# Which operand stands still in the heads' product: x as weights, 64 key columns moving

## The chip, the cores and the metric

The kernel runs on one core of a Trainium2 chip. The metric is the device time of one execution in microseconds (us); three runs of the kernel before lie at 771.75, 772.20 and 772.58 us, so its time is their median, 772.2 us. A difference of 0.2% (1.5 us) is about what a measurement of this kernel can tell from no change. Durations below come from one profiled execution, which took 773.23 us, and in which the span from the first to the last instruction was 771.4 us.

## The reference

Eight batches, each of 3200 tokens and 256 columns. First a gated attention unit, then a token-mixing MLP on its output:

```python
scores = scale * np.matmul(z, z.transpose(0, 2, 1))      # z: 3200 x 64 in each batch
attn = np.maximum(scores, 0.0) ** 2
x = u * np.matmul(attn, v)                               # 3200 x 256
wq = x @ w_q ; wk = x @ w_k                              # 3200 x 64 each
W_tok = scale2 * np.einsum('bsd,btd->bst', wq, wk)
mixed = np.einsum('bst,btd->bsd', W_tok, x)              # 3200 x 256
out = np.maximum(mixed, 0.0) @ w_out
```

`W_tok` is never made. `mixed` is `wq @ (wk.T @ x)`, and the inner product `wk.T @ x`, a 64x256 matrix for each batch, summed over its 3200 tokens, is what the kernel calls the heads (tile `hs`). The change is about how this small matrix is summed.

## The kernel before

**Work of one batch.** The 3200 tokens are 25 tiles of 128 rows. They are also grouped (`widths`) into six groups of 512 columns and one of 128. `scores` (L307) multiplies z with z into a PSUM tile of two banks (`sc`). VectorE or ScalarE takes it to SBUF with the ReLU (L321, L319), GpSimd or ScalarE squares it into `at` (L332, L330). Because the attention matrix is symmetric, part of it is not computed twice but turned by DMA (`tt`, `ts`, L351). `second_product` multiplies these tiles with v into two PSUM banks `acc0`, `acc1`. `gate` (L488) multiplies by u, which gives x of the group, in fp16. Then x is turned by DMA (`xT_sb`, L518), projected to queries and keys (`projections`, PSUM tile `qk`, copied to SBUF by ScalarE, L544), and the keys are turned by DMA into `kx` (L551): 128 tokens on the partitions, the 64 key columns beside 64 columns of zeros. `heads` multiplies keys and x, tile by tile.

**Two lanes.** Nearly all products contract over 128 rows, and the kernel runs them as two halves of 64 rows (`LOW`, `HIGH`) on the two halves of the TensorE array, called lanes here. `first_pass` gives one PSUM bank to each lane, and `second_pass` swaps the banks, so that each bank gets both halves of its rows. Class `Streams` puts the items of both lanes into one order by the columns that each lane has already moved; `swap_after` makes the second pass wait for the end of the first. In the trace these matmuls have the form 64*128 (64 rows, 128 weight columns), and a helper emits them all from L369.

**Phases.** The main loop goes in phases of some 4 us. A phase computes up to three score tiles, a share of a group's second product, and at most one more job: a mix (L622), an output projection (`fo`), or `keys_and_heads`. That last one takes one `qk` tile of two banks. Bank 0 gets the projection of a new group (two items of 512 columns in each pass). Bank 1 gets the heads of an earlier group (four items of 256 columns in each pass; five when the last, small group is among them), and sometimes the mix or the output projection of the small group (`side`), or the projection of the small group. So one lane moves 1024 columns while the other moves 1024 to 1536, and the passes swap them. `uneven` compares the two banks' columns: at the beginning of a group, banks of equal width run their two passes back to back ahead of the second product; banks of unequal width have the first pass of the second product between their own two passes. Inside a group the two passes always lie apart, with second-product work between them.

**After the product.** When the passes are done, `after` lets ScalarE copy the projections (L544) and calls `heads_out`: for the first group VectorE copies the 64x256 sum to `ha` (L576), for the next it adds (L578), and for the last it adds into the fp16 tile `hs` (L591). At the end of that phase `spread_heads` has ScalarE copy `hs` from partitions 0 to 63 to partitions 64 to 127 (L586) and into `hz` (L587), since the mix reads it on both lanes. The first mix that reads a batch's `hs` comes at least two phases later: the mix just after it in the order still belongs to the batch before.

**What sets the order.** The schedule is written by hand (`manual_schedule`): the order in which the Python code emits instructions is the order on each engine. PSUM has three tiles of two banks (pool `pps`) that `sc`, `qk`, `fo` and `mx` share in turn; the buffer given back first is handed out first. A tile's first matmul waits until the last reader of that buffer's earlier tile is done.

Of the kernel before, what the change touches and what calls it, by code (L numbers as in the profile page):

```python
# [9 lines left out]
FP16 = mybir.dt.float16  # L10
FP32 = mybir.dt.float32
# [5 lines left out]
def kernel(  # L17
# [10 lines left out]
    nc = tc.nc  # L28

    B, S, D = u.shape  # L30
    dqk = z.shape[2]
    dh = moe_w_q.shape[1]
    P = 128
# [292 lines left out]
    def second_stage(p0, g, on_act):  # L326
        at = pat.tile([P, 2 * W], FP16, tag="at", name="at")
        out = at[:].rearrange("p (a w) -> p a w", a=2)
        if on_act:
            nc.scalar.square(out=out, in_=g[:])  # L330
        else:
            nc.gpsimd.tensor_mul(out=out, in0=g[:], in1=g[:])  # L332
        blocks, turns = [], []
        for h, (b, gi, tis) in enumerate(tiles[p0 : p0 + 2]):
            for i, ti in enumerate(tis):
                made[b, gi, ti] = (at, h * W + i * widths[gi])
            gj = group_of(tis[0])
            if is_turned(gi, gj) or (gj == LASTG and gi in FOR_SMALL):
                blocks.append((b, gi, gj, tis[0] - starts[gj] // P, 1, h * W, (h + 1) * W))
        if len(blocks) == 2 and blocks[0][:3] == blocks[1][:3] and blocks[1][3] == blocks[0][3] + 1:  # L340
            blocks = [blocks[0][:4] + (2, blocks[0][5], blocks[1][6])]
        for b, gi, gj, n0, nn, c0, c1 in blocks:
            if gj == LASTG:
                turned[b, gi, gj] = ptt.tile([P, 1, 4, P], FP16, tag=f"ts{gi}", name=f"ts{gi}")
            elif (b, gi, gj) not in turned:
                home = tt_of[b, gi, gj]
                turned[b, gi, gj] = ptt.tile([P, 4, 4, P], FP16, tag=f"tt{home}", name=f"tt{home}")
            out = turned[b, gi, gj][:].rearrange("p n j t -> p (n j) t")
            turns.append(
                lambda out=out[:, 4 * n0 : 4 * (n0 + nn), :], c0=c0, c1=c1:  # L350
                nc.sync.dma_start_transpose(out=out, in_=at[:, c0:c1])  # L351
            )
        return turns
# [75 lines left out]
    def run(streams, asides_):  # L429


        todo = streams.ordered()
        total, done = sum(x[0] for x in todo), [0, 0]
        asides_ = sorted(asides_, key=lambda x: x[0])
        for n, lane, fn in todo:
            while asides_ and asides_[0][0] * total <= sum(done):
                asides_.pop(0)[1](int(done[1] < done[0]))
            fn()
            done[lane] += n
        for _, fn in asides_:  # L440
            fn(0)
# [114 lines left out]
    def swapped(gi):  # L556
        return gi % 2 == 1 or gi == LASTG

    def heads(b, gis, ps, stop=True):

        parts = [(gi, n) for gi in gis for n in range(widths[gi] // P)]
        return [
            Item(
                out=ps[:, 1, 0:D],
                lhsT=lambda r, gi=gi, n=n: ks[b, gi][r, n, :, :].rearrange("p a h -> p (a h)"),
                rhs=lambda r, gi=gi, n=n: xs[b, gi][r, n, :],
                start=((gi, n) == parts[0]),
                stop=(stop and (gi, n) == parts[-1]),
            )
            for gi, n in parts  # L570
        ]

    def heads_out(b, gis, ps):
        if gis[0] == 0:
            hacc[b] = psml.tile([P, D], FP32, tag="ha", name="ha", bufs=1)
            nc.vector.tensor_copy(out=hacc[b][0:dh, :], in_=ps[0:dh, 1, 0:D])  # L576
        elif gis[-1] < LASTG:
            nc.vector.tensor_add(  # L578
                out=hacc[b][0:dh, :], in0=hacc[b][0:dh, :], in1=ps[0:dh, 1, 0:D]
            )  # L580
        else:
            heads_done(b, ps[:, 1, 0:D], spread=False)
            to_spread.append(b)

    def spread_heads(b):
        nc.scalar.copy(out=hss[b][dh:P, :], in_=hss[b][0:dh, :])  # L586
        nc.scalar.copy(out=hz[b % 2][dh:P, :], in_=hss[b][0:dh, :])  # L587

    def heads_done(b, part, spread=True):
        hss[b] = psml.tile([P, D], FP16, tag="hs", name="hs")  # L590
        nc.vector.tensor_add(out=hss[b][0:dh, :], in0=hacc.pop(b)[0:dh, :], in1=part[0:dh, :])  # L591
        if spread:
            nc.vector.tensor_copy(out=hss[b][dh:P, :], in_=hss[b][0:dh, :])
# [158 lines left out]
    to_load = []  # L752
    todo_mix, todo_proj, todo_between, at_phase, side = [], [], [], {}, []
    keyed, keyed_at, to_turn, to_spread, asides = [], [-9], [], [], []

    def due(k, fn):
        at_phase.setdefault(k, []).append(fn)
# [19 lines left out]
    def keys_and_heads(b, gis):  # L777

        ps = ps_tile("qk")
        outs = [ps[:, 0, 0:W], ps[:, 1, D : D + P]]  # L780
        w = wkq if swapped(gis[0]) else wqk
        banks = [projections(b, gis[0], w, outs[0]), []]
        aside = None
        late = len(groups) <= NG
        heads_of = keyed[: late or len(keyed) == 2]
        if late and len(keyed) == 2 and keyed[0][0] == keyed[1][0]:
            heads_of = [(keyed[0][0], keyed[0][1] + keyed[1][1])]
            keyed[:2] = heads_of
        full = len(heads_of) == 1
        if full:  # L790
            banks[1] += heads(*heads_of[0], ps, stop=(len(gis) == 1 and not side))
            if len(gis) > 1:
                banks[1] += projections(b, gis[1], w, outs[1], start=False)
            elif side:
                aside = side.pop(0)
                banks[1] += aside[0](aside[2], ps)
        assert full or len(gis) == 1

        def after():
            for gi, o in zip(gis, outs):  # L800
                projections_out(b, gi, o)
                turn_keys(b, gi)
            if full:
                hb, hgis = keyed.pop(0)
                heads_out(hb, hgis, ps)
                if hgis[-1] == LASTG:
                    mixed_at[0] = max(mixed_at[0], now[0] - 1)
                    todo_mix.extend((hb, i, db) for i in range(LASTG // 2) for db in range(ND))
                    side.append((side_mix, side_mix_out, hb))
            if aside:  # L810
                aside[1](aside[2], ps)
            keyed.append((b, gis))
            keyed_at[0] = now[0]

        return banks, after
# [120 lines left out]
    def each(fns):  # L936
        for fn in fns:
            fn()
# [40 lines left out]
    while groups:  # L979
# [108 lines left out]
        if on_lanes:  # L1088
# [50 lines left out]
            todo = [(x, lambda lead, p0=p0: stage(p0, scores(p0, lead))) for x, p0 in zip(at_, between_)]  # L1139
            for x in acts[1:]:  # L1140
                todo.append((0.5 - 1e-6, lambda lead, x=x: each(second_stage(*x))))
            run(streams, todo)
        else:
            assert not is_split(b, gi)
# [14 lines left out]
                each(second_stage(*x))  # L1159
            for fn in matmuls[cut:]:  # L1160
                fn()
        each(late)
        ahead = []
        if closes:
# [136 lines left out]
```

## Time and profile before

| | |
|---|---|
| median of three runs | 772.2 us (771.75 to 772.58) |
| the profiled execution | 773.23 us, span 771.4 us, granted TensorE clock 0.998 |
| TensorE matmul (PE) | 760.0 us busy, 99% of the span, 12440 matmuls |
| weight loads (PEld) | 621.0 us, 81%, 12440 |
| VectorE, ScalarE, GpSimd | 466.2 (60%), 549.8 (71%), 540.2 us (70%) |
| heads' product, four-tile groups (`qk<-x_sb,kx`) | 364 matmuls, 269 ns each as recorded |
| heads' copy and adds on VectorE (L576, L578, L591) | 8 at 412 ns, 30 at 411 ns, 7 at 409 ns (and one more in the last batch) |
| spread of `hs` on ScalarE (L586, L587) | 7 at 402 ns and 7 at 398 ns |

How to read it: PE matmuls are pipelined, and the recorded 269 ns of a 256-column matmul are mostly latency; what a matmul costs is the step from its start to the start of the next one on the same lane. So PE's 99% says that it hardly waits, and not that nothing in it can be made shorter. A timeline row merges instructions of one kind; its first number is the start in us from the beginning of the span, the second the time from the first start to the last end, and x gives their number.

### The profile page before, as it was taken

The numbers are of one execution on the slowest core, as the hardware profiler recorded it, in microseconds if no ns is written. First come the engines' busy times: TensorE is split into PE (matmuls) and PEld (weight loads), VectorE is DVE, ScalarE is ACT, GpSimd is POOL, SyncE is SP. The second block draws the span as 40 slices with busy tenths as digits, with TensorE's granted clock in tenths as the row PEclk, the third lists the DMA queues.
The fourth block names the chain that finished last, engine by engine and source line by source line (L and its number), as shares of the span: only waits on it lengthen the run. The fifth ranks groups of instructions, "written<-read, shape, count | busy, mean of one in ns | idle before, by whom it ended". The sixth has DMA issues, their size and how long they took to land.

```text
span 771.4 us, 28170 instructions
## 1 busy us (share of the span) xinstructions
PE 760.0 (99%) x12440; PEld 621.0 (81%) x12440; DVE 466.2 (60%) x450; ACT 549.8 (71%) x649; POOL 540.2 (70%) x354
## 2 busy tenths in 40 slices
PE   8999999999999999999999999999999999999996
PEld 6777878788788888888888887888878888888884
DVE  6655675646765667555675557655566565765534
ACT  7566776677767867687776777768677686776555
POOL 7888797768767678666787668866688666764540
PEclk9999999999999999999999999999999999999999
DMA  8899889887999979998799997999499995889637
GB/s 169 172 197 218 198 193 179 185 172 151 201 186 216 245 140 212 204 245 189 204 189 216 227 210 156 172 235 271 118 232 203 259 225 121 176 201 191 175 74 260
DMA packets 289612, 150.19 MB, mean 195 GB/s; under 512 B 265168, under 2 KB 268752, under 8 KB 289488
## 3 DMA queue, kind: packets, MB, share of 16 engines
q1 hardware_dynamic: 288768, 146.48, 91.4%
q0 software_dynamic: 576, 1.64, 1.2%
q8 instruction: 97, 1.59, 0.9%
q14 instruction: 27, 0.22, 0.1%
q10 hardware_dynamic: 144, 0.26, 0.1%
HBM read 59.38 MB, written 26.21 MB: 111 GB/s over the span
## 4 chain that ended last, share of the span: by engine, by line
PE 97%; DVE 1%; issue 0%; DMA 0%; ACT 0%; POOL 0%; SPq 0%; ACTq 0%; DVEq 0%
PE acc L369 71%; PE sc L307 12%; PE qk L369 6%; PE fo L369 5%; PE mx L622 1%; DVE x_sb L507 1%; DMA z<-in_z_dram 0%; DVE g L321 0%; PE ztp L130 0%; PE xtx L599 0%; PE hd L609 0%; ACT g L319 0%; ACT fo L1263 0%; DVE fo L1259 0%; PE qq L369 0%
## 5 line engine op out<-in xcount | busy, mean ns | idle before, releaser
L321 DVE TENSOR_SCALAR g<-sc 128x1024 f32<-128x1024 f32 x330 | 401.7, 1223 | 243.2 <-PE sc L307 223.1
L332 POOL TENSOR_TENSOR at<-g 128x1024 f16<-128x1024 f32 x230 | 433.6, 1895 | 136.0 <-DVE g L321 113.5
L369 PE MATMUL acc<-v_sb,at 64*128 64x256 f16 (+1 forms) x7187 | 462.9, 269 | 1.5 <-DVE x_sb L507 0.5
L369 PEld LDWEIGHTS <-at 64*128 64x128 f16 (+1 forms) x7187 | 355.8, 94 | 86.8 <-PE acc L369 24.6
L330 ACT ACTIVATE at<-g 128x1024 f16<-128x1024 f32 x226 | 234.9, 1055 | 15.8 <-DMA tt<-at 8.7
L369 PE MATMUL acc<-v_sb,tt 64*128 64x256 f16 x2552 | 180.7, 269 | 0.0
L307 PE MATMUL sc<-zT 64*128 64x512 f16 (+1 forms) x1008 | 165.9, 357 | 1.4 <-ACT g L319 1.3
L319 ACT ACTIVATE g<-sc 128x1024 f32<-128x1024 f32 x126 | 129.0, 1024 | 46.5 <-PE sc L307 41.4
L369 PEld LDWEIGHTS <-tt 64*128 64x128 f16 x2552 | 130.6, 94 | 15.2
L509 POOL TENSOR_TENSOR x_sb<-gt,u_sb 128x512 f16<-128x512 f32 x48 | 61.2, 1275 | 66.2 <-ACT gt L506 58.9
L643 ACT ACTIVATE rt<-mx 128x1024 f16<-128x1024 f32 x47 | 47.9, 1024 | 34.2 <-PE mx L622 34.0
L506 ACT COPY gt<-acc 128x512 f32<-128x512 f32 x48 | 28.1, 586 | 48.6 <-PE acc L369 46.8
L307 PEld LDWEIGHTS <-zT 64*128 64x128 f16 x1008 | 52.4, 94 | 10.8 <-issue 4.2
L369 PE MATMUL fo<-wo,rt 64*128 64x256 f16 (+1 forms) x696 | 58.6, 270 | 0.0
L544 ACT CAST qk<-qk 128x512 f16<-128x512 f32 x47 | 27.5, 586 | 42.2 <-PE qk L369 39.2
L369 PE MATMUL qk<-x_sb,kx 64*128 64x256 f16 (+1 forms) x364 | 54.7, 269 | 0.0
L369 PEld LDWEIGHTS <-rt 64*128 64x128 f16 (+1 forms) x696 | 36.4, 94 | 15.0 <-PE fo L369 6.3
L507 DVE TENSOR_TENSOR x_sb<-acc,u_sb 128x512 f16<-128x512 f32 x48 | 33.2, 691 | 19.9 <-PE acc L369 19.0
L704 ACT ACTIVATE fo<-fo 128x1024 f32<-128x1024 f32 x39 | 40.0, 1026 | 2.3 <-PE fo L369 2.2
L369 PEld LDWEIGHTS <-kx 64*128 64x128 f16 (+1 forms) x382 | 35.4, 94 | 6.3 <-PE qk L369 1.2
L369 PE MATMUL qk<-xT_sb,wqk 64*128 64x512 f16 (+1 forms) x92 | 27.3, 377 | 0.0
L369 PE MATMUL qk<-xT_sb,wkq 64*128 64x512 f16 (+1 forms) x90 | 26.7, 376 | 0.0
(81 smaller groups left out, 265.6 us busy)
## 6 DMA issues: line engine op xcount, KB each, us to landing
u_sb<-in_u_dram SPq DMA_DIRECT2D x48, 512.0 KB, 5.1
out_dram<-fo SPq DMA_DIRECT2D x43, 512.0 KB, 3.6
piece<-in_v_dram SPq DMA_DIRECT2D x42, 512.0 KB, 5.2
piece<-in_z_dram SPq DMA_DIRECT2D x7, 512.0 KB, 5.6
tt<-at SPq DMA_TRANSPOSE x162, 5.0
out_dram<-fo SPq DMA_DIRECT2D x9, 256.0 KB, 3.4
piece<-in_z_dram SPq DMA_DIRECT2D x7, 288.0 KB, 4.5
u_sb<-in_u_dram SPq DMA_DIRECT2D x8, 128.0 KB, 3.8
```

The source lines that it names most:

```text
L307: nc.tensor.matmul(out=sc[:, h, at : at + w], lhsT=zT[b][half : half + dqk, ds(z_at(b, h) + ti * P, P)], rhs=zT[b][half : half + dqk, ds(z ...
L319: nc.scalar.activation(out=g[:], in_=sc[:], func=RELU, scale=GSCALE)
L321: nc.vector.tensor_scalar(out=g[:], in0=sc[:], scalar1=0.0, scalar2=GSCALE, op0=AOP.max, op1=AOP.mult)
L330: nc.scalar.square(out=out, in_=g[:])
L332: nc.gpsimd.tensor_mul(out=out, in0=g[:], in1=g[:])
L369: return nc.tensor.matmul(out=self.out, lhsT=self.lhsT(rows), rhs=self.rhs(rows), start=start, stop=stop)
L506: nc.scalar.copy(out=upper[:], in_=accs[1][:])
L507: nc.vector.tensor_mul(out=x[:, 0:n], in0=accs[0][:, 0:n], in1=ug[:, 0:n])
L509: nc.gpsimd.tensor_mul(out=x[:, n : 2 * n], in0=upper[:], in1=ug[:, n : 2 * n])
L544: nc.scalar.copy(out=qks[b, gi][:, 0:gw], in_=out)
L643: nc.scalar.activation(out=out, in_=ps[:], func=RELU)
L704: nc.scalar.mul(out=flat_out[:, sl], in_=part, mul=FINAL_SCALE)
```

## The change

In all batches but the last (`b < last`) the operands of the heads' product change places. For each token tile x is the weights, in two blocks of 128 columns (`cc`), and the 64 key columns move. The output is then x's columns on the partitions and the heads on the free axis: 128 partitions, two blocks of 64 columns. `ha` becomes 128x128. For the last groups of a batch VectorE adds the sum twice into an fp16 tile `hT`, once for each of two copies of the 64 columns (`t`). A new function `turn_heads` multiplies `hT` by the identity, two products of 128 rows, 128 weight columns and 128 moving columns, which puts the heads on partitions 0 to 63 and again on 64 to 127. They go into columns 256 to 511 of the same `qk` tile's second bank, and ScalarE copies the 128x256 result to `hs`. `turn_heads` is put at the end of the phase's stream of second-product items. `spread_heads` keeps only the copy to `hz`. The last batch is computed as before.

```diff
     def heads(b, gis, ps, stop=True):
         parts = [(gi, n) for gi in gis for n in range(widths[gi] // P)]
+        if b < last:
+            return [
+                Item(
+                    out=ps[:, 1, ds(cc * dh, dh)],
+                    lhsT=lambda r, gi=gi, n=n, cc=cc: xs[b, gi][r, n, ds(cc * P, P)],
+                    rhs=lambda r, gi=gi, n=n: ks[b, gi][r, n, 0, :],
+                    start=((gi, n, cc) == parts[0] + (0,)),
+                    stop=(stop and (gi, n, cc) == parts[-1] + (ND - 1,)),
+                )
+                for gi, n in parts
+                for cc in range(ND)
+            ]
         return [
...
     def heads_out(b, gis, ps):
+        cols, n = (P, ND * dh) if b < last else (dh, D)
+        part = ps[0:cols, 1, 0:n]
         if gis[0] == 0:
-            hacc[b] = psml.tile([P, D], FP32, tag="ha", name="ha", bufs=1)
-            nc.vector.tensor_copy(out=hacc[b][0:dh, :], in_=ps[0:dh, 1, 0:D])
+            hacc[b] = psml.tile([P, n], FP32, tag="hT" if b < last else "ha", name="ha", bufs=1)
+            nc.vector.tensor_copy(out=hacc[b][0:cols, :], in_=part)
         elif gis[-1] < LASTG:
-            nc.vector.tensor_add(
-                out=hacc[b][0:dh, :], in0=hacc[b][0:dh, :], in1=ps[0:dh, 1, 0:D]
-            )
-        else:
-            heads_done(b, ps[:, 1, 0:D], spread=False)
-            to_spread.append(b)
+            nc.vector.tensor_add(out=hacc[b][0:cols, :], in0=hacc[b][0:cols, :], in1=part)
+        else:
+            hT = psml.tile([P, ND, 2, dh], FP16, tag="h16", name="hT")
+            for t in range(2):
+                nc.vector.tensor_add(
+                    out=hT[:, :, t, :],
+                    in0=hacc[b][:].rearrange("p (a h) -> p a h", a=ND),
+                    in1=part.rearrange("p (a h) -> p a h", a=ND),
+                )
+            hacc.pop(b)
+            hTs[b] = hT
+
+    def turn_heads(b, hT, ps):
+        for cc in range(ND):
+            nc.tensor.matmul(
+                out=ps[:, 1, ds(D + cc * P, P)],
+                lhsT=hT[:, cc, :, :].rearrange("p t h -> p (t h)"),
+                rhs=ident[:],
+                start=(cc == 0),
+                stop=(cc == ND - 1),
+            )
+        hss[b] = psml.tile([P, D], FP16, tag="hs", name="hs")
+        nc.scalar.copy(out=hss[b][:], in_=ps[:, 1, D : 2 * D])
+        to_spread.append(b)
 
     def spread_heads(b):
-        nc.scalar.copy(out=hss[b][dh:P, :], in_=hss[b][0:dh, :])
-        nc.scalar.copy(out=hz[b % 2][dh:P, :], in_=hss[b][0:dh, :])
+        nc.scalar.copy(out=hz[b % 2][dh:P, :], in_=hss[b][dh:P, :])
...
     def keys_and_heads(b, gis):
         assert full or len(gis) == 1
+        if full and heads_of[0][0] < last and heads_of[0][1][-1] == LASTG:
+            assert not aside and len(gis) == 1
+            hb_ = heads_of[0][0]
+            to_turn_heads.append(lambda: turn_heads(hb_, hTs.pop(hb_), ps))
...
             for x in acts[1:]:
                 todo.append((0.5 - 1e-6, lambda lead, x=x: each(second_stage(*x))))
+            if to_turn_heads:
+                streams.aside(max(streams.at), to_turn_heads.pop(0))
             run(streams, todo)
...
             for fn in matmuls[cut:]:
                 fn()
+        while to_turn_heads:
+            to_turn_heads.pop(0)()
         each(late)
```

More of the change, by code (lines that the diff above doesn't have):

```diff
@@ L754 @@
     keyed, keyed_at, to_turn, to_spread, asides = [], [-9], [], [], []
+    hTs, to_turn_heads = {}, []
     def due(k, fn):
```

## The prediction

> **What bounds the kernel now.** I read the page first, then who waits on PE, then the timeline of PE in narrow windows, since the change is about matmuls of a shape that the kernel does not have yet.
>
> ```profile
> PE 760.0 (99%) x12440; PEld 621.0 (81%) x12440; DVE 466.2 (60%) x450; ACT 549.8 (71%) x649; POOL 540.2 (70%) x354
> ...
> PE 97%; DVE 1%; issue 0%; DMA 0%; ACT 0%; POOL 0%; SPq 0%; ACTq 0%; DVEq 0%
> ...
> L369 PE MATMUL qk<-x_sb,kx 64*128 64x256 f16 (+1 forms) x364 | 54.7, 269 | 0.0
> ```
>
> The chain that ends last is PE for 97%. The longest entry of PE in the view of waits is 1.3 us in all. So whatever the two lanes save or lose is the kernel's time, nearly one to one. What a matmul costs is the step to the next one on its lane:
>
> ```profile
> 84.13 0.60 PE L307 MATMUL sc<-zT 64*128 64x128 f16 x10
> 84.57 0.60 PE L369 MATMUL acc<-v_sb,at 64*128 64x256 f16 x8
> ...
> 86.31 0.38 PE L307 MATMUL sc<-zT 64*128 64x512 f16 x2
> 86.54 1.48 PE L369 MATMUL acc<-v_sb,at 64*128 64x256 f16 x24
> 87.86 0.60 PE L369 MATMUL acc<-v_sb,tt 64*128 64x256 f16 x8
> 88.30 0.38 PE L307 MATMUL sc<-zT 64*128 64x512 f16 x2
> ```
>
> From 86.54 to 87.86, 12 pairs (one matmul on each lane): 110 ns a step; the single start times of the trace give 109. In the row at 84.13 the ten are four pairs of 128 columns and one of 512: 0.44 us less 0.216 for the 512 leaves 56 ns a step, and each of these steps also loads new weights on both lanes. The line through 109 at 256 and 56 at 128 columns gives 29.5 ns at 64. At 86.31 the step after 512 columns is 0.23 instead of 0.216: by the start times 228 against 216 where the next weights were not loaded ahead, and the recorded time of the matmul after it is 280 instead of 269. So a weight load that nothing hides costs 12 to 23 ns.
>
> ```profile
> 676.99 0.38 PE L369 MATMUL qk<-xT_sb,wqk 64*128 64x512 f16 x1
> 677.12 0.28 PE L369 MATMUL qk<-x_sb,kx 64*128 64x256 f16 x1
> 677.21 0.38 PE L369 MATMUL qk<-xT_sb,wqk 64*128 64x512 f16 x1
> 677.24 0.38 PE L369 MATMUL qk<-x_sb,kx 64*128 64x256 f16 x2
> 677.42 0.27 PE L369 MATMUL acc<-v_sb,at 64*128 64x256 f16 x1
> ```
>
> The lanes are independent: the second projection starts 215 ns after the first though heads emitted ahead of it are not started, and the lane that is through with its share goes on with the second product (677.42). So a shorter heads' share is not lost to the longer projection beside it, as long as there is second-product work behind it, and over the two passes each lane gets the short share once.
>
> **What the change removes.** 25 tiles in 7 batches, 175 tiles, each once on each lane. A tile's share of a lane is 109 ns now, and two matmuls of step t after: 109 - 2t saved, 175 times. Bounds for t: from below 29.5, the line above, weights loaded in the shadow of 64 columns. From above 29.5 + 23 = 52.5, no load hidden, or 56, the narrowest step that the trace shows. Saved: 8.75 us at 29.5; 0.7 us at 52.5; -0.5 us at 56. I take 32: the load of 12 to 23 ns fits into the 27 ns that 64 columns take at the line's slope, the other lane then needs a load only every 109 or 215 ns, and a few first loads of a run will be late. 109 - 64 = 45 ns, 175 times: **7.9 us saved**.
>
> The Trainium skill speaks against that: its page "TensorE: Matmul & The Clock Gate", section LDWEIGHTS, gives a load 1/1.2 ns for each weight column, 107 ns for 128 whatever the rows, and its section on weight-path modes reports about half of that as measured with fast weight load. By 53 ns a load the step would be bound at some 53 to 56 ns and the sum would come out near +2.6 us, the loss priced below as a rival. The trace excludes 107 (a step with a load on each lane in 56 ns), and cannot exclude 53.
>
> **What it adds on PE.** `turn_heads`, seven times: two 128-row matmuls of 128 columns, 56 ns each. They stand among 64-row matmuls, and that switch has a price:
>
> ```profile
> 52.16 0.38 PE L307 MATMUL sc<-zT 64*128 64x512 f16 x2
> 52.47 0.60 PE L369 MATMUL qk<-xT_sb,wqk 128*128 128x512 f16 x2
> 53.01 0.39 PE L307 MATMUL sc<-zT 64*128 64x512 f16 x2
> ```
>
> 0.31 us from a 512-column pair to the 128-row matmul, against 0.216: 97 ns by the start times, and the same back (0.54 less 0.43). 2 x 0.056 + 2 x 0.097 = 0.31 us, seven times 2.1 us. Does PE also wait for `hT`? Two ends of the tail after the heads:
>
> ```profile
> 331.66 0.59 ACT L544 CAST qk<-qk 128x512 f16<-128x512 f32 x1 [0.92 <-PE qk L369]
> ...
> 332.28 0.41 DVE L591 TENSOR_TENSOR hs<-ha,qk 64x256 f16<-64x256 f32 x1 [0.21 <-ACT qk L544]
> ...
> 333.19 0.38 PE L622 MATMUL mx<-qk,hs 64*128 64x512 f16 x2
> ```
>
> The add starts when ScalarE's cast is done. An add of 128 columns has no row; from 0.411 at 256 and 0.691 at 512 columns on VectorE the line gives 0.27 us. Two adds from 332.28 end at 332.82, with 0.06 for the semaphore 332.88; PE reaches the end of the phase at 333.19. The four batches from the third to the sixth have this spare of 0.3 us; the second (add at 242.80, end of phase 243.57) 0.2; the first more than 1 us. The seventh has none:
>
> ```profile
> 679.08 0.59 ACT L544 CAST qk<-qk 128x512 f16<-128x512 f32 x1 [1.07 <-PE qk L369]
> 679.70 0.41 DVE L591 TENSOR_TENSOR hs<-ha,qk 64x256 f16<-64x256 f32 x1
> ...
> 679.86 0.48 PE L307 MATMUL sc<-zT 64*128 64x512 f16 x2
> ```
>
> There `hT` is ready at 679.70 + 0.54 + 0.06 = 680.30, and everything behind the turn on PE waits from 679.86: 0.45 us once. **Added: 2.6 us.** Bounds: 0.8 us if the switch cost nothing (only 14 steps of 56 ns), and 7.5 us if every turn also stopped what follows (third rival).
>
> **What moves beside it.** The `qk` buffer is held until ScalarE has copied the turned sum: 0.22 us matmul time (the 128-column row), 0.05, the copy 0.38 (a 128x256 read from PSUM takes 373 and 384 ns in the rows of L499 and L728), 0.06: 0.7 us after the turn. It is the buffer given back last, so two tiles go first. In the third to sixth batch the third tile comes at 335.37, 2 us after; in the second it is the closest, 0.65 us after plus the switch back, some 0.1 us to spare. On ScalarE 0.40 (L586) goes and 0.38 comes, but later: the copy now waits for the turn, and the copy to `hz`, the z spread and the mix's ReLU queue behind it, up to 0.8 us later. The mix's PSUM buffer is wanted again at 337.36, while its ReLU ended at 335.21: cover enough, and 0.5 us a batch if it were gone. The first mix that reads the new `hs` is two or more phases away. VectorE's 35 copies and adds of 0.41 become 0.27, and seven more are added: 60% busy, nothing. No DMA is added, and no issue of SP or POOL is moved past another. In five keying phases at a group's beginning (96.3, 110.9, 138.7, 198.9 and 78.9 us) the banks were equal and now are not, so the second product's first pass goes between their passes; four phases run this way already (124.9, 152.7, 293.7, 481.2) without a wait on PE: 0, within 0.3 us each way, 1.5 us in all.
>
> **Sum.** -7.9 + 2.6 = -5.3 us on the profiled 773.23 (span 771.4 and 1.8 around it). The profiled run lies 1.0 above the median, and the difference is carried over to it: 772.2 - 5.3 = **766.9 us**.
>
> **Rivals.**
> - *Weight loads bind* (slower). Twice as many loads, each with only 64 columns to hide behind, on PEld that is 81% busy. Steps of 52.5 to 56 ns save 0.7 to -0.5 us against 2.6 added: 774.1 to 775.3 us. It decides from t = 47, where 175 x (109 - 94) is the 2.6 that the turn costs. For it: the exposed load of up to 23 ns, close to the 27 ns of 64 columns. Against it: at 128 columns no load shows at all. The Trainium skill's rule above is this case: by 53 ns a load it gives 774 to 775.
> - *Half hidden*: t about 40 saves 5.1, less 2.6: 769.7.
> - *The turn is waited for*: a scores tile behind each turn needs the buffer and waits 0.7 us, seven times 4.9: 771.8 at t = 32. For it: 0.1 us to spare in the second batch. Against it: 2 us in four others.
> - *DMA takes over*: the gain goes into late transposes, near 772.
>
> ```profile
> 358.00:452.00 94.00, 93.84 (x1578) 76.63 (x1574) 58.30 (x55) 69.19 (x82) 69.62 (x43) 1.00 1.00 209
> ```
>
>   The share of the 16 DMA engines (last but one) is 1.00 over a whole batch. But shares overlap, PE has no wait on a DMA, and the profile's slices of DMA dip to 4 tenths.
>
> **How the numbers follow.** Forecast 0.48 (765.0 to 768.7, t from 29.5 to 36 and the group-begin phases), half hidden 0.14, turn waited for 0.10, loads bind 0.22, DMA 0.06. Faster by over 0.2%: 0.48 + 0.14 + 0.03 of the third = 0.65. Within 0.2%: 0.04 of the third and 0.04 of DMA, 0.08. Slower: 0.22 + 0.03 + 0.02 = 0.27. The range takes in the first two, the third and the lower half of loads-bind: 765.0 to 774.6.
>
> **What would show it.** The row `qk<-kx,x_sb` with some 700 matmuls of 64x64, in runs with a step near 30 ns on a lane (right), or 40, or over 47 (wrong: loads bind). Seven pairs of 128-row matmuls with 0.1 us of gap on either side, ScalarE's copy behind each, and a gap of 0.45 us ahead of the seventh. PE's waits still near zero for `sc` behind the turns; more would be the third rival. L578 at 0.27 us. The prediction fails above all if t does.

## The result, and the profile after

The changed kernel takes 768.75 us (median of six runs, 768.06 to 769.64), the kernel before 772.0 us measured beside it. The ratio is 0.9956 with a 95% interval of 0.9944 to 0.9969: 3.25 us faster, where 5.3 us had been forecast. The profiled run of the changed kernel is 768.53 us with a span of 766.8. The two profiled executions differ by more, 4.7 us. Of that, 1.3 us is there by the scores matmul at 43 us, while the first heads' product comes at 78 us: the profiled run of before waited in this opening 0.4 us for POOL's `zd` and about 1 us for ScalarE's `g`. From that matmul to the start of the last one, before takes 720.5 us and the changed kernel 716.7, a gain of 3.7 us. The time behind the last matmul, in which the output is written, was 0.4 us longer in the changed kernel's profiled run, so that 3.3 us are left in the span, in line with the medians.

The page of the changed kernel, first the busy row and the chain, then the groups of the new products (operation, shapes, count, busy us, mean ns of one, idle before):

```profile
PE 755.3 (99%) x12804; PEld 618.0 (81%) x12804; DVE 462.0 (60%) x457; ACT 549.7 (72%) x649; POOL 540.0 (70%) x354
...
PE 96%; DVE 2%; issue 1%; DMA 0%; ACT 0%; DVEq 0%; ACTq 0%; SPq 0%
...
L369 PEld LDWEIGHTS <-x_sb 64*128 64x128 f16 x672 | 30.2, 95 | 4.2 <-PE qk L369 0.2
L369 PE MATMUL qk<-kx,x_sb 64*128 64x64 f16 x672 | 32.7, 190 | 0.0
```

PE is still the chain's 96%, so the sum is still to be made on its two lanes. Of the 364 products of 256 columns, 336 have become 672 of 64, with as many loads (the other 28 are the last batch's). What one of them costs is not the 190 ns of the row (that is how long one matmul is under way) but the step to the next on its lane. The timeline of PE in a keying phase of the second batch:

```profile
237.67 0.19 PE L369 MATMUL qk<-kx,x_sb 64*128 64x64 f16 x1
237.67 0.38 PE L369 MATMUL qk<-xT_sb,wkq 64*128 64x512 f16 x1
237.69 0.36 PE L369 MATMUL qk<-kx,x_sb 64*128 64x64 f16 x7
237.89 0.38 PE L369 MATMUL qk<-xT_sb,wkq 64*128 64x512 f16 x1
```

Seven matmuls of 0.19 us each occupy 0.36 us: six steps in 0.17 us, 28 ns; the single start times of the trace give 29.2. So a tile takes 58 ns of a lane instead of 109. Summed over a whole lane by steps (215.5, 109.2, 55.7 and 29.2 ns for 512, 256, 128 and 64 columns), the matmuls need some 738 us, 8.1 less than before: 175 x (109.2 - 58.4) = 8.9 us less for the heads, and 14 steps of 56 ns more for the turns. The other side of the sum is the time in which a lane stands still between two matmuls. It grew by 4.4 us (the mean of the two lanes) once the 1.3 us of the opening are set aside: 8.1 less 4.4 is the gain of 3.7.

Three places hold most of that growth. One is the turn, here the second batch's:

```profile
240.73 0.71 PE L369 MATMUL acc<-v_sb,tt 64*128 64x256 f16 x9
240.87 0.28 DVE L598 TENSOR_TENSOR hT<-ha,qk 128x128 f16<-128x128 f32 x1
...
241.37 0.28 PE L610 MATMUL qk<-ident,hT 128*128 128x128 f16 x2
...
241.59 0.39 PE L307 MATMUL sc<-zT 64*128 64x512 f16 x2
241.69 0.37 ACT L618 CAST hs<-qk 128x256 f16<-128x256 f32 x1 [1.37 <-PE qk L610]
```

The last second-product matmul starts at 241.17, its step ends at 241.28; the turn starts at 241.37 and the scores at 241.59. That is the predicted 0.31 us, two steps of 56 and two switches of some 97 ns.

The second is a keying phase at a group's beginning. The kernel before:

```profile
110.83 0.69 DVE L507 TENSOR_TENSOR x_sb<-acc,u_sb 128x512 f16<-128x512 f32 x1
110.85 0.38 PE L369 MATMUL qk<-xT_sb,wqk 64*128 64x512 f16 x1
110.85 0.38 PE L369 MATMUL qk<-x_sb,kx 64*128 64x256 f16 x2
110.92 0.59 ACT L506 COPY gt<-acc 128x512 f32<-128x512 f32 x1 [1.20 <-PE acc L369]
...
111.96 1.47 PE L369 MATMUL acc<-v_sb,at 64*128 64x256 f16 x24
```

and the changed kernel:

```profile
109.43 0.69 DVE L507 TENSOR_TENSOR x_sb<-acc,u_sb 128x512 f16<-128x512 f32 x1
109.51 0.58 ACT L506 COPY gt<-acc 128x512 f32<-128x512 f32 x1 [1.20 <-PE acc L369]
109.66 0.38 PE L369 MATMUL qk<-xT_sb,wqk 64*128 64x512 f16 x1
109.66 0.39 PE L369 MATMUL qk<-kx,x_sb 64*128 64x64 f16 x8
109.88 0.38 PE L369 MATMUL qk<-xT_sb,wqk 64*128 64x512 f16 x1
...
110.15 2.12 PE L369 MATMUL acc<-v_sb,at 64*128 64x256 f16 x35
```

`gate` reads the accumulators of the group that has ended: ScalarE's copy until 110.10, VectorE's product until 110.12. Before, both extra passes stood in front of the second product and lasted until 111.96, so the gate (over at 111.52) was covered. Now only one pass stands in front. The heads' lane is through at 109.90 and starts its first `acc` matmul at 110.15, 50 ns after ScalarE is done: 255 ns idle. Behind the second extra pass, the lane that had the heads in it stands still as well (217 ns, until 112.80).

The third is new in the waits of PE:

```profile
PE qk L369 <- DMA kx<-ql: 0.7, 1, 0.7
```

On SP's queue:

```profile
668.68 1.17 SPq L551 DMA_TRANSPOSE kx<-ql  x1
```

At 671.1 the heads of the seventh batch reach the small group's tile, whose keys SP began to transpose at 668.68. They land at 672.0, and both lanes stand still for 0.84 and 0.96 us.

### The profile page after: what moved, and what is told of

It reads as the page before. It is cut to its first block, busy times and chain, and to the rows that moved or that the text cites. A ratio compares the mean times of both kernels' runs of the same rounds, so it can differ in the third digit from the quotient of the medians.

```text
span 766.8 us, 28900 instructions
## 1 busy us (share of the span) xinstructions
PE 755.3 (99%) x12804; PEld 618.0 (81%) x12804; DVE 462.0 (60%) x457; ACT 549.7 (72%) x649; POOL 540.0 (70%) x354
## 3 DMA queue, kind: packets, MB, share of 16 engines
q1 hardware_dynamic: 288768, 146.48, 92.6%
## 4 chain that ended last, share of the span: by engine, by line
PE 96%; DVE 2%; issue 1%; DMA 0%; ACT 0%; DVEq 0%; ACTq 0%; SPq 0%
PE acc L369 72%; PE sc L307 12%; PE fo L369 5%; PE qk L369 4%; PE mx L657 1%; DVE x_sb L507 1%; DVE g L321 0%; DMA kx<-ql 0%; DVE fo L1303 0%; PE sc L972 0%; PE ztp L130 0%; PE qk L610 0%; PE xtx L634 0%; ACT at L330 0%; PE hd L644 0%
## 5 line engine op out<-in xcount | busy, mean ns | idle before, releaser
L369 PEld LDWEIGHTS <-at 64*128 64x128 f16 (+1 forms) x7187 | 352.1, 94 | 87.2 <-PE acc L369 24.0
L369 PEld LDWEIGHTS <-x_sb 64*128 64x128 f16 x672 | 30.2, 95 | 4.2 <-PE qk L369 0.2
L369 PE MATMUL qk<-kx,x_sb 64*128 64x64 f16 x672 | 32.7, 190 | 0.0
```

What stands on the lines that cost most here:

```text
L369: return nc.tensor.matmul(out=self.out, lhsT=self.lhsT(rows), rhs=self.rhs(rows), start=start, stop=stop)
```

## The experiments

A step or a phase is compared below from trace to trace (from one scores matmul's start to a later one's), since the whole time varies by some 0.5 us from run to run. Two stretches vary though nothing is changed in them: the opening, up to the scores matmul at 43 us (42.1 to 43.9 us in these traces), and the time behind the start of the last matmul (6.5 to 7.5 us). What lies between the two is called the middle below: 720.5 us before, 716.7 in the changed kernel. The changed kernel's 768.75 us is the measure where the kernel before is not named.

### The old order in the five begin phases

```
     def uneven(extra):
-        return a != b
+        return a != b and b != W
...
-                marks = [max(streams.at)]
+                marks = [sum(x[2] for x in streams.todo)]
...
```

> The changed kernel, with the five group-begin keying phases put back to the order of before (both passes of the extra product ahead of the second product), a scores tile between the two passes. Theory A (the begin phases eat part of the gain: the heads' lane is through its 512 columns 0.25 us before the gate has emptied the accumulators, and at the end of the second extra pass the lane idles another 0.22 us): these five phases get back 0.44 to 0.48 us each, 2.2 us in all, so about 766.5 us (766.2 to 767.3) against 768.75 for the changed kernel. Theory B (the begin phases cost nothing, as the prediction had it; the gain was lost elsewhere): 768.75 within 0.3 us. A third outcome: the swap between the passes makes the short lane wait for the long one, 0.22 us a phase, and the order of before gains only 1 us: 767.7.

Measured: 768.33 us, ratio to before 0.9953 (0.9941 to 0.9965). Theory A, that the changed order as such costs 2.2 us, falls; 768.33 is also just outside theory B's range, and the third outcome has the right stop at more than twice its worth. Here is the phase at 109 us in this kernel's timeline of PE:

```profile
109.49 0.38 PE L369 MATMUL qk<-xT_sb,wqk 64*128 64x512 f16 x1
109.50 0.39 PE L369 MATMUL qk<-kx,x_sb 64*128 64x64 f16 x8
109.71 0.38 PE L369 MATMUL qk<-xT_sb,wqk 64*128 64x512 f16 x1
109.73 0.57 PE L307 MATMUL sc<-zT 64*128 64x512 f16 x2
110.14 0.20 PE L369 MATMUL qk<-kx,x_sb 64*128 64x64 f16 x1
110.15 0.39 PE L369 MATMUL qk<-xT_sb,wqk 64*128 64x512 f16 x1
```

The gate no longer shows, but the heads' lane (0.23 us of heads, then its half of the scores from 109.73 to 109.95) waits until 110.15 for the swap, that is for the other lane's projections to end: 204 ns. It stands still again for 0.21 us behind the next scores tile, until 112.78. The old order loses at the swaps what the new one loses at the gate. Elsewhere this run has a wait that the changed kernel's does not have:

```profile
PE acc L369 <- DVE gt L500: 0.3, 1, 0.3
```

At 183 us the second product waits for the small group's gate, and that phase is 0.37 us longer. So the middle is 716.8 us, no shorter than the changed kernel's.

### The turn left out

```
-        for cc in range(ND):
-            nc.tensor.matmul(
-                out=ps[:, 1, ds(D + cc * P, P)],
...
-        nc.scalar.copy(out=hss[b][:], in_=ps[:, 1, D : 2 * D])
+        nc.scalar.copy(out=hss[b][:], in_=ps[:, 0, 0:D])
```

> The changed kernel without the two identity products of the turn (the turning back is left out; hs is filled by a copy of the same size from the projections' bank). Theory A: the turn costs 7 x 0.31 us (two steps of 56 ns and two changes of row mode of 97 ns) and 0.2 us of waiting for hT in the seventh batch, 2.3 us in all: 766.4 us (766.1 to 766.8) against 768.75. Theory B (the turn is where the missing 2 us went, by drains or waits that the steps do not show): 4.5 us or more come back, 764.3 or below.

Measured: 766.0 us, ratio 0.9928 (0.9916 to 0.9941), 2.75 us less than with the turn. In the trace six turns are worth 0.32 to 0.34 us each and the seventh about 0.5, together 2.5 us, so theory A holds. The middle is 3.2 us shorter (713.6), and the rest of that is not the turn: in this run the small group's keys were there in time, and the wait at 672 us (0.8 us of the stretch) was missing.

### The turn on two lanes

```
         for cc in range(ND):
-            nc.tensor.matmul(
-                out=ps[:, 1, ds(D + cc * P, P)],
-                lhsT=hT[:, cc, :, :].rearrange("p t h -> p (t h)"),
-                rhs=ident[:],
...
+            for lane, r in enumerate((LOW, HIGH)):
+                nc.tensor.matmul(
+                    out=ps[:, lane, ds(D + cc * dh, dh)],
+                    lhsT=hT[r, cc, :, :].rearrange("p t h -> p (t h)"),
+                    rhs=ident[r, ds(lane * dh, dh)],
...
```

> The changed kernel with the turn made in the 64-row mode: one half of the rows on each lane, against half of the identity, 64 columns, into two banks. Theory A (the price of a turn is mostly the change of row mode, 2 x 97 ns): a turn shrinks from 0.31 us to two steps of 29 ns on each lane, 0.25 us less, seven times 1.7 us: 767.0 us (766.8 to 767.5) against 768.75. Theory C (PE would have waited there anyway, for hT or for the drain of what is ahead): the gap stays whatever the mode, 768.6 within 0.3 us.

Measured: 766.26 us, ratio 0.9925 (0.9913 to 0.9937). The timeline, at the same place as the turn shown above:

```profile
240.46 1.04 PE L369 MATMUL acc<-v_sb,tt 64*128 64x256 f16 x16
240.73 0.48 DVE L598 TENSOR_TENSOR hT<-ha,qk 128x128 f16<-128x128 f32 x2
...
241.33 0.22 PE L611 MATMUL qk<-ident,hT 64*128 64x64 f16 x4
241.39 0.38 PE L307 MATMUL sc<-zT 64*128 64x512 f16 x2
```

From the turn's first matmul to the scores it is 0.06 us, and in six turns nothing is lost ahead of it. These six are 0.26 to 0.27 us shorter each, and the seventh 0.12, since it still waits 0.30 us for `hT`. In the second batch 0.13 us of the gain goes into a stop ahead of the scores tile at 244.85. The middle is 1.7 us shorter (715.0), the median 2.5; the traces do not show where the other 0.8 us lie. Theory A holds: of the 0.33 us of a turn, 0.26 to 0.27 were change of row mode, and it was not needed.

### All 128 key columns

```
-                    out=ps[:, 1, ds(cc * dh, dh)],
+                    out=ps[:, 1, ds(cc * P, P)],
...
-                    rhs=lambda r, gi=gi, n=n: ks[b, gi][r, n, 0, :],
+                    rhs=lambda r, gi=gi, n=n: ks[b, gi][r, n, :, :].rearrange("p a h -> p (a h)"),
...
```

> The changed kernel with all 128 key columns moving (the upper 64 of them zeros) instead of 64: as many weight loads as the changed kernel, twice the columns, and every extra product as wide as in the kernel before, so that its phases keep the order of before. Theory A: 175 tiles by (2 x 55.7 - 109.2) = +0.4 us, the turn +2.3 us, nothing else: 774.7 us (774.3 to 775.2) against 772.0 of the kernel before. Theory B (the turn or the doubled weight loads cost more than the single steps show): 776.5 or above. Against the changed kernel it says what the 64 columns and the altered phases are worth together: by A 6.0 us, of which 175 x 2 x 26.5 ns = 9.3 us is the columns, and 2.3 is lost in phases whose passes became unequal and 0.9 in a wait for a transpose of keys.

Measured: 775.71 us, ratio 1.005 (1.0038 to 1.0062), 1.0 us above theory A and below theory B. Two waits that theory A had not counted make up that 1.0 in the trace: 0.7 us for the small group's keys, and the 0.37 us at 183 us seen with the old order. It is the cleanest view of what the 64 columns are worth in each kind of phase, since weight loads and turns are equal. The lengths of phases, in us (each from one scores matmul to a later one, the first five around the begin phases, the last an ordinary keying phase at 125 us):

```
phase at, us          78     96    111    139    199   ordinary
before              5.49   7.87   5.50   5.50   5.17       5.62
changed             5.52   7.70   5.55   5.55   5.22       5.41
128 key columns     5.52   7.90   5.53   5.53   5.20       5.62
old order           5.48   7.84   5.48   5.48   5.15       5.41
```

An ordinary phase gets the full 0.21 us (four tiles by 2 x 26.5 ns). Four of the five begin phases get nothing from half the columns in the new order, and 0.04 to 0.05 us in the old one. The fifth, at 96 us, gets 0.17 against the kernel before in the new order and 0.03 in the old one. It follows the small group, whose accumulators are another pair of reads (256 columns each) and free earlier. That points to the gate. It also corrects the sum: these phases lose their own gain, about 0.23 us in four of them, not the 0.45 us that the first theory had read from the idle times of single lanes.

The run shows too that the wait for `kx<-ql` (0.5 us in its view of waits, 0.7 on the heads' lane) is not all due to the heads' speed: with 128 columns the heads are about as long as before, and wait.

### The scores tiles moved into the stops

```
                 first_extra = first_pass(streams, extra[0], across)
+                marks = [sum(x[2] for x in streams.todo)]
                 first = first_pass(streams, banks, across)
                 extra_second(first_extra)
+                marks.append(sum(x[2] for x in streams.todo))
                 second_pass(streams, first)
+                total = sum(x[2] for x in streams.todo)
+                at_ = [(x - 1) / total for x in marks][: len(between_)]
```

> The changed kernel, in the order it has for unequal passes, but with the two scores tiles of such a phase put elsewhere: one behind the first extra pass (where the heads' lane waits for the gate to empty the accumulators), one behind the second extra pass (where it stood ahead of it, and the lanes' swap waited for it to end). Theory D (in four of the five begin phases the lanes stand still twice, 0.25 us for the gate and 0.22 us at the swap, and other work can fill both): the mean of the two lanes' idle time, 0.23 to 0.30 us a phase, goes to below 0.1: 4 x 0.2 = 0.8 us, and up to 0.3 more in the four phases that ran in this order already: 767.7 us (767.4 to 768.0) against 768.75. Theory B (unequal shares are waited for somewhere in any order, as the order of before showed with 768.33): 768.3 to 768.8.

Measured: 768.64 us, ratio 0.9952 (0.9939 to 0.9964). Theory B had it. The timeline of PE:

```profile
109.07 0.38 PE L307 MATMUL sc<-zT 64*128 64x512 f16 x2
109.29 0.38 PE L369 MATMUL qk<-xT_sb,wqk 64*128 64x512 f16 x1
109.29 0.39 PE L369 MATMUL qk<-kx,x_sb 64*128 64x64 f16 x8
109.50 0.38 PE L369 MATMUL qk<-xT_sb,wqk 64*128 64x512 f16 x1
109.52 0.57 PE L307 MATMUL sc<-zT 64*128 64x512 f16 x2
109.99 0.40 PE L369 MATMUL acc<-v_sb,at 64*128 64x256 f16 x4
```

The scores follow the heads at once, but the idle stretch has only moved behind them: the heads' lane is through with its half of the scores at 109.74 and goes on at 109.99 or just after. The stop at the swap is gone, and one lane leaves the phase 0.18 us ahead of the other, for which it then waits at the next swap (until 116.97). So the phase is only 0.05 us shorter (5.50 instead of 5.55), and the middle 0.2 (716.6). From the phase's first scores matmul to the first `acc` matmul it is 0.92 us here (109.07 to 109.99), and in the changed kernel 0.92 us too (109.23 to 110.15). The gate sets that time. Moving a tile from ahead of the heads to behind them brings no more work into its shadow.

### A shorter gate

```
+            short = (b, gi) in ((0, 4), (1, 0), (1, 2), (2, 0))
+            m = D if short else n
...
-                nc.scalar.copy(out=upper[:], in_=accs[1][:])
+                nc.scalar.copy(out=upper[:, 0:m], in_=accs[1][:, 0:m])
-            nc.vector.tensor_mul(out=x[:, 0:n], in0=accs[0][:, 0:n], in1=ug[:, 0:n])
+            nc.vector.tensor_mul(out=x[:, 0:m], in0=accs[0][:, 0:m], in1=ug[:, 0:m])
...
```

> The changed kernel with a shorter gate ahead of four begin phases (78, 110, 137 and 198 us): it reads only the first half of each accumulator (the gated values of the other half are left out, other data of the same size stand in for them), so that the accumulators are free some 0.25 us earlier. Theory D: the second product's first matmuls start within 0.05 us of the end of the heads' first pass instead of 0.25 us after it, and each of the four phases gets 0.13 to 0.17 us shorter, 0.5 to 0.7 us in all: 768.15 us. The stop at the swap stays. Theory B (the gate is not what holds these matmuls, or its wait is only moved to the swap): 768.75 within 0.2 us.

Measured: 768.03 us, ratio 0.9942 (0.9929 to 0.9954). The timeline:

```profile
109.71 0.59 PE L307 MATMUL sc<-zT 64*128 64x512 f16 x4
109.91 0.43 DVE L509 TENSOR_TENSOR x_sb<-acc,u_sb 128x256 f16<-128x256 f32 x1
110.00 0.37 ACT L508 COPY gt<-acc 128x256 f32<-128x256 f32 x1 [1.20 <-PE acc L369]
110.14 0.38 PE L369 MATMUL qk<-xT_sb,wqk 64*128 64x512 f16 x1
110.15 0.39 PE L369 MATMUL qk<-kx,x_sb 64*128 64x64 f16 x8
...
110.42 0.81 PE L369 MATMUL acc<-v_sb,at 64*128 64x256 f16 x10
```

ScalarE's copy ends at 110.37 and the heads' lane goes on at 110.42, 42 ns after its last heads step. From the first scores matmul it is 0.71 us instead of 0.92. All four phases are 0.21 us shorter (5.55 to 5.34 twice, 5.52 to 5.31, 5.22 to 5.01), as much as ordinary phases gain, and the middle is 0.55 us shorter (716.2). The stop at the swap shrinks by itself, from 217 to 81 ns. So in this order the gate is what holds the gain of these phases: shown by shortening it. It is more than theory D asked for (0.13 to 0.17 each), which had charged part of it to the swap.

### The keys' transposes ahead

```
         for x in acts[:1]:
-            each(second_stage(*x))
+            (late.extend if k == 150 else each)(second_stage(*x))
```

> The changed kernel with one transpose on SP's queue (tt, in the phase at 663 us) put behind the two transposes of the keys that it stood ahead of, so that these are issued 1.3 us earlier. Theory A (the heads of the seventh batch now come before the keys of the small group have landed, 0.85 to 0.96 us on both lanes at 672 us): that wait is gone and nothing else is late, 767.9 us (767.7 to 768.2) against 768.75. Rival: the transpose that is put back, or the turn behind the heads, which then waits for VectorE's adds, takes up part of it: 768.3 or above.

Measured: 767.58 us, ratio 0.994 (0.9926 to 0.9954). SP's queue in this kernel:

```profile
664.70 1.23 SPq L518 DMA_TRANSPOSE xT_sb<-x_sb  x1
666.02 1.20 SPq L551 DMA_TRANSPOSE kx<-qk  x1
667.33 1.17 SPq L551 DMA_TRANSPOSE kx<-ql  x1
668.55 1.30 SPq L351 DMA_TRANSPOSE tt<-at  x1
```

The keys' transpose starts at 667.33 instead of 668.68, the wait is gone, and 0.79 us of it stays gained (the stretch from 676 to 680 us of before's time is 4.04 us instead of 4.83). The middle is 0.8 us shorter too (716.0). One transpose ahead of another on a queue was worth a quarter of the whole change.

### Three of these together

The turn on lanes, the moved scores tiles and the keys ahead, each edited as above.

> The turn on the two 64-row lanes, the scores tiles of the unequal begin phases moved, and the keys' transposes ahead, all three together. The turn on lanes alone gave 766.26. With 0.85 us from the keys and 0.8 us from the begin phases: 764.6 us (764.2 to 765.3), 1.0% under the kernel before. If the begin phases give nothing: 765.4.

Measured: 766.37 us, ratio 0.9921 (0.9909 to 0.9934): no less than with the turn on lanes alone (766.26). In the trace the middle is 714.2 us, 0.86 less than with the turn on lanes alone (715.0), nearly all of it the keys' wait. The opening, where nothing is changed, was 1.4 us longer in the profiled run than the changed kernel's. With five runs each the medians do not tell these two kernels apart. Both beat the kernel before and the changed one.

### Everything into the gate's shadow

The old order in all nine unequal begin phases before the last batch, and the tile that stood ahead of the phase put between the extra's passes too:

```
-        return a != b
+        return a != b and groups[0][0] == last
...
+            if begins and keying and groups[0][0] < last: heading = 0
...
+                if len(between_) == 3: marks = marks[:1] + marks
```

> The changed kernel with all nine keying phases at a group's beginning (before the last batch) in this order: heads and projections, two scores tiles, the extra's second passes, the second product's first pass, a scores tile, its second pass. So both extra passes and all three scores tiles but one stand in the shadow of the gate, and on the short lane two tiles instead of one stand ahead of the swap. Theory D (the gate's shadow and the swap each have to be filled with other work, and there is enough if all of it is put there): the five phases become 0.2 us shorter each, as the shorter gate made four of them, and the four others 0.1: 768.75 - 1.2 = 767.5 us (767.2 to 767.9). Theory E (moved work is missed where it stood, as when the scores tiles were moved with 768.64): 768.5 within 0.4 us.

Measured: 771.21 us, ratio 0.999 (0.9981 to 0.9998), 2.5 us worse than the changed kernel; the middle is 720.5 us, as long as before. Theory D's mechanism shows in three of the phases (0.17, 0.17 and 0.13 us shorter in all). In others there is a price that the expectation had not named. It stands in this kernel's waits of PE:

```profile
PE sc L307 <- DVE ha L594: 1.6, 2, 0.8
PE sc L307 <- ACT g L319: 1.3, 3, 0.5
```

Scores wait for VectorE's add of the heads in the phases at 296 and 481 us, 0.8 us in each, and both phases are 0.9 us longer. The likely reason: the `qk` buffer and three scores tiles are four tiles for three PSUM buffers, and a scores tile gets the buffer of `qk` only when the add has read it. In the phases at 78 and 154 us scores wait 0.5 and 0.4 us for ScalarE's first stage of an earlier tile (`g`; the third of these waits is in the opening), and the phases are 0.6 and 0.5 us longer. The rest of the loss lies outside: 0.4 us at 183 us, as with the old order, 0.2 at 367 us, and 0.8 about the seventh batch's keys, which landed later still than in the changed kernel.

The same order with the turn on lanes and the keys ahead:

> That order with the turn on the two lanes and the keys' transposes ahead. Alone, the turn on lanes gave 1.9 us in the steps of its trace (6 x 0.28 and 0.12) and the keys 0.8: 768.75 - 1.8 - 0.8 - 1.2 = 765.0 us by theory D, 766.1 by theory E.

Measured: 768.47 us, ratio 0.9954 (0.9942 to 0.9967). That is 2.1 us above the version with the scores tiles moved (766.37), about what the 771.21 against 768.64 would have it; the middle is 717.5 us against 714.2.

And with the seventh turn put behind the next phase's first scores tile:

```
+            if to_turn_heads and b == last:
+                turn_next.append(to_turn_heads.pop(0))
...
         fresh = [(p0, scores(p0)) for p0 in pairs]
+        while turn_next:
+            turn_next.pop(0)()
```

> The same, and the seventh turn put behind the next phase's first scores tile, so that PE does not wait for VectorE's adds there (0.30 us on both lanes in every run so far): 0.2 to 0.3 us less than without: 764.7 us by theory D, 765.8 by theory E. If the buffer that the turn now holds longer is missed by the next scores tile, no less than without.

Measured: 768.82 us, ratio 0.9957 (0.9945 to 0.997). The stretch with the seventh turn is 0.37 us shorter (3.52 instead of 3.89), and two later ones are 0.15 and 0.24 longer: the wait was only moved.

### Twice the loads for the same columns

```
...
-                    rhs=lambda r, gi=gi, n=n: ks[b, gi][r, n, 0, :],
+                    rhs=lambda r, gi=gi, n=n, q=q: ks[b, gi][r, n, 0, q : q + 32],
...
                 for cc in range(ND)
+                for q in (0, 32)
```

> The changed kernel with each heads product of 64 key columns in two of 32, each with its own weight load: twice the loads, the same columns. It tells how close 29 ns a step is to what loads allow. If loads hide behind 32 columns too, a step is about 16 ns by the line through 55.7 ns at 128 and 29.2 at 64 columns, and 175 tiles lose 4 x 16 - 58 = 6 ns each: 769.8 us. If a load on one lane needs some 29 ns, so that 64 columns just cover it, a tile takes 4 x 29: 175 x 58 ns = 10.2 us more: 779 us. If a load needs 23 ns (the longest exposed load that the trace of before showed): 4 x 23 - 58 = 34 ns a tile, 774.7 us.

Measured: 776.72 us, ratio 1.0055 (1.004 to 1.0071). Columns of the timeline as before:

```profile
472.69 0.18 PE L369 MATMUL qk<-kx,x_sb 64*128 64x32 f16 x1
472.70 0.38 PE L369 MATMUL qk<-xT_sb,wqk 64*128 64x512 f16 x1
472.72 0.45 PE L369 MATMUL qk<-kx,x_sb 64*128 64x32 f16 x12
```

Twelve matmuls of 0.18 us in 0.45 us are eleven steps of 25 ns; the start times give 25.1. By 175 x (4 x 25.1 - 58.4) that is 7.4 us, and 8.0 were measured (9.2 in the middle, 726.0 us; the difference is not explained). So 32 columns do not go faster than 25 ns a step, and the 29.2 ns of 64 columns lie only 4 ns above that bound. Whether it is the load that binds there or each matmul's own start, this run doesn't tell. The Trainium skill, "TensorE: Matmul & The Clock Gate", section "Wait — 56ns, not 53.3ns?", says that the distance of two starts does not fall below about 25 ns however few columns there are; the 25.1 agrees, and then a load needs no more than that.

## Why the prediction was right in direction and too large by 2 us

**The step t**, the one the forecast hung on, had the right mechanism: 29.2 ns, just under the lower bound of 29.5 from the line through 109 and 56, not the 32 taken. The 23 ns of an unhidden load vanish behind 27 ns of columns, also on the first steps of a run (single steps are 28 to 30 ns, one is 38). The heads are worth 8.9 us instead of 7.9. The rivals "weight loads bind" and "half hidden" are out. By the rule of the Trainium skill that the prediction cites ("TensorE: Matmul & The Clock Gate", section LDWEIGHTS: 107 ns for 128 columns, or about half with fast weight load) a step could not be 29 ns if one load on a lane follows the other; the trace has 672 such matmuls at 29.2 ns a step, and 25 ns in the last experiment.

**The turn**, 2.6 us: right in sum, 2.5 us by its steps (14 x 56 ns and 1.75 us of idle time) and 2.5 by leaving it out. The switch is 92 to 96 ns each way, close to the 97 read from the opening. The seventh waits 0.2 us for `hT` (0.45 forecast), the others not at all. What the prediction did not ask is whether the switch was needed: half the rows on each lane do the same for 0.06 us. The Trainium skill states the rule, "TensorEngine Tiling (Array Packing)", section Key Properties: a change of tiling mode drains the array. Here the change costs the 92 to 96 ns.

**The five begin phases**, "0, within 0.3 us each way, 1.5 us in all": the bound held and the value failed. The two lanes' mean idle time there is 1.0 us more (0.23 to 0.25 us in four of the phases), and 0.1 more in the phases that ran unequal before. The sentence that failed is the one on independent lanes, "as long as there is second-product work behind it". At a group's beginning there is none until the gate has read the accumulators. The four phases that the prediction took as its model showed 0.05 to 0.12 us of idle time on a lane at that place, too short for the view of waits; in the first of them, at 125.44, the second product starts 60 ns after VectorE's product is done. It was kept small by heads that still took 109 ns a tile.

**A wait that the prediction did not list**: the keys of the small group, 0.9 us. "No issue of SP is moved past another" was true and not enough. The phase had no slack: in the kernel before, the heads of that phase already stood still for 0.17 us there, and reached the small tile 2.9 us after its transpose was issued; now they reach it 2.4 us after, and the transpose lands after 3.3. So about half of the wait is that the heads come earlier after the issue, and half that the keys land late; with 128 columns, where the tile is reached after 2.7 us, PE waits too. The seven runs of the changed kernel and its variants in which this transpose keeps its place and PE waits 0.7 us or more had it land 3.2 to 3.9 us after issue; with the turn left out, and with 32 columns, it was there by 2.3 us. Why it lands late in one run and in time in another is open.

**The other rivals.** No scores tile waited for the turned `qk` buffer, and no transfer took over: the share of the main DMA queue rose from 91.4 to 92.6% with no other wait of PE on a DMA.

The sum of the parts: -8.9 for the heads, +2.5 for the turn, +1.1 for begin phases, +0.9 for the keys, and +0.7 that is left in stops of 20 to 80 ns in many phases, not examined one by one: -3.7, as the middle shows. The longer writing of the output in the profiled run makes it -3.3 in the span, and the medians have -3.25. Against the forecast of -5.3, the heads gave 1.0 more, and 2.7 us went into stops that were costed at nothing. That the result came as near as 2 us to the forecast is in part luck, since the two errors have opposite signs; and the range of 765.0 to 774.6 holds a loss as well as a gain, so that lying in it says little.

## What to carry to other kernels

A lane or an engine that is made faster keeps its gain only where work that is ready stands behind it: for each place of the gain, look for the next thing that its follower waits for (here the reading of the accumulators), and cost the gain up to that point. Idle time on one lane is not the price of a stop, since a scores tile put into the stop left the phase nearly as long as it was and the wait came behind it; what counts is the time between the events that bound it. And before a product is put into another row mode, see whether its rows can be split over the lanes instead.

## What the runs showed of the hardware

- A 64-row matmul of 64 columns with its own load of 128 weight columns takes 29.2 ns a step on its lane while the other lane streams 512 columns; with 32 columns 25.1 ns.
- A change between the 64-row and the 128-row mode costs 92 to 96 ns each way, in six turns alike.
- Matmuls on one lane start ahead of earlier ones on the other: in the phase at 112 us a second-product matmul that comes after a scores matmul of the other lane in the program started 87 ns before it (112.242 against 112.329).
- The transpose of one small group of keys took from 2.3 to 4.2 us from issue to landing in one execution.
